# Folding layer norm's centring and gain into the first weight matrix, with every weight set multiplied by Strassen's scheme

## The chip, the cores and the metric

The kernel runs on one core of one Trainium2 chip. The metric is the device time of one execution in microseconds (us). Each kernel is run several times; the median counts.

## The reference

Attention without softmax, whose output x goes through a feed-forward part with a residual. There are 8 batches of 448 tokens, 12 heads of 64, 768 channels and 3072 hidden units.

```python
scores = (1/sqrt(64)) * q @ k.T                 # each batch and head
x      = (maximum(scores, 0)**2 / 448) @ v      # heads side by side: (8, 448, 768)
mu, var = mean(x, -1), mean((x - mu)**2, -1)
xn     = (x - mu) / sqrt(var + 1e-6) * g_ln     # g_ln > 0, one value for each channel
out    = x + maximum(xn @ w_ch1, 0) @ w_ch2     # 768 -> 3072 -> 768
```

Inputs and output are float32; the products run in bf16 and add up in float32.

## The kernel before

**Pairs and stages.** The 8 batches are worked in 4 pairs of 896 tokens (seven token tiles of 128, `NT`). For each pair x is kept transposed, `xT`: six chunks (`K1`) of 128 channels on the partitions, tokens along the free axis. `xc` is the centred x times g, one tile for each batch. The hidden layer is `hT`, 24 chunks (`K2`) of 128 hidden units by 896 tokens. Dividing by the standard deviation is left to the end: a token's `rstd` is positive, so it can be multiplied on after both products.

The stages follow each other on TensorE: pair 0's attention together with pair 0's first product (x to hidden); then three times a *loop*, in which a pair's second product (hidden to output) is interleaved with the next pair's attention, followed by that next pair's first product; last the second product of pair 3.

**Attention in a loop.** `attention` makes a list of units: bundles of three score tiles (L335 on TensorE, relu on ScalarE L346, square on VectorE L348), with `values` (L365) put in once a group of four heads is complete. `values` evicts x from PSUM (L372), scales it by g (`scaled`, L388), and `chunks_summed` (L400 to L407) adds up the six chunks of x on GpSimd. `centre` multiplies by a matrix of ones (L421), so that every partition holds each token's sum over the channels, and adds -g/768 times it to `xc` (L427).

**The second product.** `ffn2` (L634) has 56 units a pair: 7 token tiles, 2 halves of the output columns, 4 parts of 6 matmuls with 384 columns. After the fourth part `finish` (L645) multiplies by `rstd`, adds x and `store` sends the result out on SyncE's queue. `tokens` turns `xT` into token rows by a DMA transpose (L565); `statistics` (L572) and `roots` (L577, ScalarE's square root, then a reciprocal on VectorE) make `rstd` one tile ahead. `interleave` spreads the bundles over the units.

**The first product of pair 0** goes in blocks of 192 or 256 columns (`BLK`), so that it can begin before attention is done: `ffn1_head` (L618) takes the first three hidden chunks, `ffn1` (L596) each of the other 21, in two PSUM banks (`ps_mm`) used in turn, with a relu on ScalarE (L604). The last block is the 192 columns of batch 1 (`b=1`); it has no attention beside it.

**The first product of pairs 1 to 3** (`ffn1_pair`). Strassen's scheme multiplies two 2 x 2 block matrices with 7 block products instead of 8. The blocks are: hidden chunk n or n+12, channel chunks 0 to 2 or 3 to 5 (`KQ` = 3), batch `lo` or `hi` of the pair. A *set* n is thus 7 products of 3 matmuls with 448 columns (L752), against 24 plain matmuls, and needs five sums of w1 blocks and five sums of x blocks. Ten of the twelve sets go this way. The other two are plain, 48 matmuls (L596, the list `beside`): they give time for the x sums (`x_sum`, x[6], x[7]) and for the first sets' w1 sums. Those are made by GpSimd (`sums_early`, L721 to L723) and VectorE (`sums_late`, L735 and L739), two sets ahead. While pair 2 does this it also stores its sums in DRAM (`kept`, L744); pair 3 reads them back (`w_soon` L710 on ScalarE's or SyncE's queue, `w_late` L730 on SyncE's).

**What sets the order.** The program order is the schedule: each engine works through its instructions in the order written, waiting on semaphores for what it needs. Pools with few buffers add waits: `ps_sc` has 3 buffers of two banks, `ps_mm` 2 banks, `xc` 2 tiles, `ps_m` (first product, while `ps_sc` is closed) 6 banks. `busy` (L310) and `idle` (L206) are matmuls whose result nobody uses.

Of the kernel before, what the change touches and what calls it, by code (L numbers as in the profile page):

```python
# [28 lines left out]
def kernel(  # L29
# [156 lines left out]
    g_rows = const.tile([K1, 2, HP], fp32)  # L186
# [115 lines left out]
    FIRST = (0, BLK[0][0])  # L302
# [24 lines left out]
    def scores(n, slots, blk):  # L327
# [19 lines left out]
        if blk == FULL:  # L347
            nc.vector.tensor_mul(a, a, a)  # L348
        else:
            later.append((n, a))  # L350
# [3 lines left out]
    def values(n, blk):  # L354
# [15 lines left out]
        if b not in xc:  # L370
            xc[b] = xcpool.tile([P, K1, S], bf16, tag="xc", name="xc_sb")
        nc.vector.tensor_scalar_mul(  # L372
            xT[b // 2][:, 2 * m:2 * m + 2, of(blk, b)], ps[:, :, :w], score_scale)
        if (b, blk) != FIRST:
            scaled(b, m, blk)
        g["attn"] = []
        since[0] = 9
        if blk == FULL:
            chunks_summed(b, m)
# [10 lines left out]
    part = {}  # L390

    def chunks_summed(b, m):


        x = xT[b // 2][:, :, of(FULL, b)]
        if b % 2 and m == G - 1:
            return
        if m == 0:
            part[b] = spool.tile([P, S], fp32, tag="total", name="part_sb", bufs=1)
            nc.gpsimd.tensor_add(part[b], x[:, 0], x[:, 1])  # L400
        else:
            for c in range(2 * m, 2 * m + 2):
                nc.gpsimd.tensor_add(part[b], part[b], x[:, c])  # L403
        if m == G - 1 - b % 2:
            two = spool.tile([P, 2, S], bf16, tag="two", name="two_sb", bufs=1)
            nc.gpsimd.tensor_copy(two[:, 0], part[b])
            nc.gpsimd.tensor_sub(two[:, 1], part[b], two[:, 0])  # L407
            part[b] = two

    def centre(b, blk):  # L410
        w = blk[1] * HP
        straight = (b, blk) == FIRST or blk == FULL and b % 2
# [4 lines left out]
        rows = [xT[b // 2][:, c, of(blk, b)] for c in range(K1)]  # L417
        if blk == FULL:
            rows = [part[b][:, i] for i in range(2)] + (rows[4:] if b % 2 else [])
        for i, r in enumerate(rows):  # L420
            nc.tensor.matmul(ps, ones, r, start=(i == 0), stop=(i == len(rows) - 1))  # L421
        total = ps
        if not straight:
            total = spool.tile([P, S], fp32, tag="total", name="total_sb", bufs=1)[:, :w]
            nc.scalar.copy(total, ps)
        for c in range(K1):
            nc.vector.scalar_tensor_tensor(  # L427
                xc[b][:, c, of(blk)], total, g_mean[:, c:c + 1], xc[b][:, c, of(blk)],
                op0=ALU.mult, op1=ALU.add)

# [91 lines left out]
    def attention(bs):  # L522
# [9 lines left out]
        def item(n, i):  # L532
            scores(n, (i,), FULL)
            if i == J - 1 and n + 3 < len(groups):
                transposed(n + 3)

        def product(n):
            values(n, FULL)
            load(n + 4, "v")

        def bundle(items, at):
            for o, it in enumerate(items):
                item(*it)
                if o == at:
                    product(it[0] - 1)
        units, due = [], [[], []]
        for s in range(0, len(seq), 3):
# [4 lines left out]
            due.append([groups[n][0]] if at >= 0 and groups[n][1] == G - 1 else [])  # L552
            units += [lambda b=b: centre(b, FULL) for b in due.pop(0)]
        units.append(lambda: product(hi - 1))
        units.append(lambda: centre(bs[-1], FULL))
        return units
# [28 lines left out]
    def ffn1(b, ni, blk, few=False):  # L585
# [5 lines left out]
        if few:  # L591
            ps = ps_m.tile([P, 512], fp32, tag="m", name="h_ps")
        else:
            ps = ps_mm.tile([P, 512], fp32, tag="mm", name="h_ps")
        for c in range(K1):
            nc.tensor.matmul(  # L596
                ps[:, :w], w1[:, c, ni * P:(ni + 1) * P], xc[b][:, c, of(blk)],
                start=(c == 0), stop=(c == K1 - 1))
        since[0] += 1
        turns = 2 if (b, blk) == FIRST else 1  # L600
        if blk != FULL and since[0] <= turns:
# [6 lines left out]
    def ffn1_head(b, blk):  # L608
# [5 lines left out]
        one = ps_mm.tile([P, 512], fp32, tag="mm", name="h_ps")[:, :w]  # L614
        two = ps_sc.tile([P, 2, 512], fp32, tag="sc", name="h2_ps")[:, :, :w]
        for c in range(K1):
            for ni, ps in enumerate((one, two[:, 0], two[:, 1])):
                nc.tensor.matmul(  # L618
                    ps, w1[:, c, ni * P:(ni + 1) * P], xc[b][:, c, of(blk)],
                    start=(c == 0), stop=(c == K1 - 1))  # L620
# [42 lines left out]
    def ffn1_pair(pair, rows, beside, keep=False, given=None, between=None):  # L663
# [5 lines left out]
        lo, hi = xc[2 * pair], xc[2 * pair + 1]  # L669
        x = {3: lo[:, :KQ], 4: hi[:, KQ:], 6: hi[:, :KQ], 7: lo[:, KQ:]}  # L670
        w = {}
        first = spool.tile([P, 2, S], bf16, tag="two", name="w1_sum", bufs=1)
        first = first.rearrange("p i s -> p (i s)")
        temps = [spool.tile([P, S], fp32, tag="total", name="z_sb", bufs=1), first.bitcast(fp32)]
        if given is None:
            hold_x = [apool.tile([P, 2, 512], bf16, tag="attn", name="x_sum")[:, :, :S] for _ in range(5)]
            for m, t, rest in ((5, 0, (3, 0)), (2, 1, (3, 1)), (1, 2, (4, 0))):
                x[m] = (hold_x[t], hold_x[t][:, 0], hold_x[t][:, 1], hold_x[rest[0]][:, rest[1]])
            w_room = [[apool.tile([P, 2, 512], bf16, tag="attn", name="w1_sum")
                       .rearrange("p r (c n) -> p (r c) n", n=P) for _ in range(2)] for _ in range(2)]  # L680
            room = xpool.tile([P, K1, S2], bf16, tag="xT", name="room_sb")
            rest = room[:, KQ:].rearrange("p c s -> p (c s)")[:, :2048].rearrange("p (c n) -> p c n", n=P)
            w_room.append([rest[:, :8], rest[:, 8:]])
        else:
            for i, m in enumerate((5, 2, 1)):
                o = given["x"][:, i * KQ * S:(i + 1) * KQ * S].rearrange("p (c s) -> p c s", s=S)
                x[m] = (o, o[:, 0], o[:, 1], o[:, 2])
            room = xpool.tile([P, K1, S2], bf16, tag="xT", name="room_sb")
        temps += [room[:, n].bitcast(fp32) for n in range(KQ)]

        def x_sum(m, a, b):
            if given is None:
                nc.vector.tensor_add(x[m][0], a[:, :2], b[:, :2])
                nc.vector.tensor_add(x[m][3], a[:, 2], b[:, 2])
            else:
                nc.vector.tensor_add(x[m][0], a, b)

        def blocks(n):
            i, j = rows[n]
            i, j = slice(i * P, (i + 1) * P), slice(j * P, (j + 1) * P)  # L700
            return w1[:, :KQ, i], w1[:, :KQ, j], w1[:, KQ:, i], w1[:, KQ:, j]

        def sums_early(n):
            if n >= len(rows):
# [3 lines left out]
            if given is not None:  # L708
                soon = given["pool"].tile([P, 3 * KQ, P], bf16, tag="soon", name="w1_soon", bufs=2)
                (nc.scalar if n > 1 else nc.sync).dma_start(soon, kept[:, n, :3 * KQ])  # L710
                w[n].update({3: soon[:, :3], 4: soon[:, 3:6], 1: soon[:, 6:9]})
                return
            one, two = w_room[n % 3]
            if n == 0:
                f = first.rearrange("p (c n) -> p c n", n=P)
                w[n].update({3: f[:, :3], "4a": f[:, 3:5], "4b": f[:, 5], 4: f[:, 3:6]})
            else:
                w[n].update({3: two[:, :3], "4a": one[:, 6:8], "4b": two[:, 6],
                             4: (None, one[:, 6], one[:, 7], two[:, 6])})
            w[n].update({1: one[:, :3], 6: one[:, 3:6], 7: two[:, 3:6], "16": one[:, :6]})  # L720
            nc.gpsimd.tensor_sub(w[n][3], b12, b22)  # L721
            nc.gpsimd.tensor_sub(w[n]["4a"], b21[:, :2], b11[:, :2])
            nc.gpsimd.tensor_sub(w[n]["4b"], b21[:, 2], b11[:, 2])  # L723

        def sums_late(n):
            if n >= len(rows):
                return
            if given is not None:
                late = given["pool"].tile([P, 2 * KQ, P], bf16, tag="late", name="w1_late", bufs=2)
                nc.sync.dma_start(late, kept[:, n, 3 * KQ:])  # L730
                w[n].update({6: late[:, :3], 7: late[:, 3:6]})
                return
            b11, b12, b21, b22 = blocks(n)
            j = slice(rows[n][1] * P, (rows[n][1] + 1) * P)
# [5 lines left out]
            if keep:  # L740
# [14 lines left out]
        def relu(n, ps, row, half):  # L755
            nc.scalar.activation(  # L756
                hT[pair][:, rows[n][row], half * S:(half + 1) * S], ps, ACTF.Relu)
# [10 lines left out]
        for unit in beside[:4]:  # L768
            unit()
        sums_early(0)  # L770
        sums_early(1)
        if given is not None:
            sums_late(0)
            sums_late(1)
            tokens(pair)
        x_sum(5, lo[:, :KQ], lo[:, KQ:])
        x_sum(2, hi[:, :KQ], hi[:, KQ:])
        x_sum(1, lo[:, :KQ], hi[:, KQ:])
# [362 lines left out]
```

## Time and profile before

Three runs took 526.82 us in the median (526.72 to 527.58). The profiled execution took 527.49 us; its span, from the first to the last instruction in the trace, is 525.7.

| engine | busy us | share of the span | instructions |
|---|---|---|---|
| TensorE, matmuls (PE) | 516.9 | 98% | 4612 |
| TensorE, weight loads (PEld, beside the matmuls) | 305.5 | 58% | 4612 |
| VectorE (DVE) | 388.5 | 74% | 727 |
| ScalarE (ACT) | 284.1 | 54% | 478 |
| GpSimd (POOL) | 197.3 | 38% | 246 |

The stages, from the times of their first and last instructions:

| stage | from, us | to, us | PE busy in it |
|---|---|---|---|
| attention and first product of pair 0, without its last block | 0 | 88.7 | 84.5 |
| last block of pair 0's first product | 88.7 | 100.0 | 11.2 |
| loop 0: second product of pair 0, attention of pair 1 | 100.0 | 175.2 | 75.2 |
| first product of pair 1 | 175.2 | 225.9 | 50.7 |
| loop 1 | 225.9 | 299.2 | 73.3 |
| first product of pair 2 | 299.2 | 350.2 | 51.0 |
| loop 2 | 350.2 | 423.4 | 73.2 |
| first product of pair 3 | 423.4 | 474.7 | 51.0 |
| second product of pair 3 | 474.7 | 525.7 | 46.8 |

A row of a profile names an engine, a source line (L752 is line 752 of the kernel), the operation, the tile written and the tiles read with the shape. Times are in microseconds from the start of the span. SP is SyncE, which here only issues DMAs.

### The profile page before, as it was taken

Reading aid. Unit: us, or ns where it says so; the run is one execution under the profiler, and the core shown is the slowest. Engines: PE = TensorE matmul, PEld = TensorE weight load, DVE = VectorE, ACT = ScalarE, POOL = GpSimd, SP = SyncE. Lnnn points to the kernel's source line nnn. Section 1 sums busy time; section 2 is a strip of 40 time slices with the busy share of each in tenths; the row PEclk is TensorE's granted clock in tenths of the full one; section 3 lists DMA queues with packets and bytes.
Section 4 is the critical chain, followed back from the end, with each engine's and each line's share of the span. In section 5 each row is a group of like instructions: output and inputs, shape, how many; then the busy total and the mean of one; then the engine's idle time right before and its main releaser. Section 6 shows DMA issues by size and latency. Waiting matters only on the chain.

```text
span 525.7 us, 11571 instructions
## 1 busy us (share of the span) xinstructions
PE 516.9 (98%) x4612; PEld 305.5 (58%) x4612; DVE 388.5 (74%) x727; ACT 284.1 (54%) x478; POOL 197.3 (38%) x246
## 2 busy tenths in 40 slices
PE   8899999999999999999999999999999999999996
PEld 6678778755555555555555555555555554555663
DVE  5775654278898788758889779856989856886773
ACT  6966775465545266746646256647555435761110
POOL 7335102114624376002343727300330319991331
PEclk9999999999999999999999999999999999999999
DMA  9999999999988930216999885614651147421123
GB/s 196 206 206 207 211 192 164 172 159 139 171 137 153 185 68 0 36 31 102 169 170 179 134 206 172 157 36 62 131 104 46 46 111 185 116 88 31 38 54 91
DMA packets 121224, 66.50 MB, mean 126 GB/s; under 512 B 79698, under 2 KB 119890, under 8 KB 121170
## 3 DMA queue, kind: packets, MB, share of 16 engines
q1 hardware_dynamic: 92178, 37.05, 36.2%
q0 software_dynamic: 26976, 25.50, 33.0%
q10 hardware_dynamic: 2016, 3.21, 1.7%
q8 instruction: 36, 0.59, 0.5%
q14 instruction: 18, 0.15, 0.1%
HBM read 56.82 MB, written 15.93 MB: 138 GB/s over the span
## 4 chain that ended last, share of the span: by engine, by line
PE 93%; DMA 3%; POOL 2%; ACT 1%; DVE 1%; issue 0%; ACTq 0%; DVEq 0%; POOLq 0%
PE o_ps L634 34%; PE m_ps L752 21%; PE h_ps L596 15%; PE m_ps L885 8%; PE sc_ps L335 7%; PE av_ps L365 6%; DMA w<-in_moe_w_ch_dram 2%; PE h_ps L618 1%; DMA w_soon<-kept 1%; PE sum_ps L421 1%; ACT early L346 1%; PE tr_ps L220 1%; POOL v_sb L130 0%; POOL w L148 0%; POOL k_sb L130 0%
## 5 line engine op out<-in xcount | busy, mean ns | idle before, releaser
L634 PE MATMUL o_ps<-w,hT_sb 128*128 128x384 bf16 x1056 | 181.6, 326 | 0.0
L346 ACT ACTIVATE attn_sb<-sc_ps 128x896 bf16<-128x896 f32 (+4 forms) x150 | 126.4, 902 | 82.3 <-PE sc_ps L335 69.5
L634 PEld LDWEIGHTS <-hT_sb 128*128 128x128 bf16 x1056 | 99.6, 98 | 78.1 <-issue 15.2
L348 DVE TENSOR_TENSOR attn_sb<-attn_sb 128x896 bf16<-128x896 bf16 x126 | 81.6, 662 | 31.5 <-ACT attn_sb L346 26.9
L756 ACT ACTIVATE hT_sb<-m_ps 128x448 bf16<-128x448 f32 x120 | 65.2, 544 | 37.7 <-PE m_ps L752 35.7
L596 PE MATMUL h_ps<-xc_sb,w 128*128 128x192 bf16 (+2 forms) x648 | 82.2, 280 | 0.7 <-DMA w<-in_moe_w_ch_dram 0.3
L596 PEld LDWEIGHTS <-w 128*128 128x128 bf16 x648 | 58.1, 98 | 20.9 <-issue 3.1
L604 ACT ACTIVATE hT_sb<-h_ps 128x192 bf16<-128x192 f32 (+2 forms) x93 | 37.7, 406 | 56.8 <-PE h_ps L596 56.3
L400 POOL TENSOR_TENSOR part_sb<-xT_sb 128x448 f32<-128x448 bf16 x6 | 6.6, 1103 | 104.6 <-DVE xT_sb L372 84.9
L403 POOL TENSOR_TENSOR part_sb<-part_sb,xT_sb 128x448 f32<-128x448 f32 x18 | 23.3, 1295 | 55.6 <-DVE xT_sb L372 54.9
L846 POOL TENSOR_TENSOR w_sum_t<-w 128x384 bf16<-128x384 bf16 x48 | 41.8, 910 | 0.0
L752 PE MATMUL m_ps<-x_sum,w 128*128 128x448 bf16 x180 | 38.9, 352 | 0.0
L752 PE MATMUL m_ps<-xc_sb,w_sum 128*128 128x448 bf16 x168 | 36.4, 352 | 0.0
L572 DVE BATCH_NORM_STATS2 stats<-xtok_sb 128x6 f32<-128x384 bf16 x56 | 28.3, 546 | 10.7 <-DMA xtok_sb<-xT_sb 10.7
L335 PE MATMUL sc_ps<-qT_sb,kT_sb 64*64 64x448 bf16 x504 | 35.0, 358 | 0.0
L372 DVE TENSOR_SCALAR xT_sb<-av_ps 128x896 bf16<-128x896 f32 (+2 forms) x30 | 27.0, 901 | 7.8 <-PE av_ps L365 7.7
L365 PE MATMUL av_ps<-attn_sb,v_sb 64*64 64x448 bf16 (+2 forms) x672 | 32.3, 327 | 0.0
L752 PEld LDWEIGHTS <-w_sum 128*128 128x128 bf16 x210 | 20.5, 98 | 19.3 <-issue 0.3
L645 DVE SCALAR_TENSOR_TENSOR o_sb<-o_ps,rstd_sb,xtok_sb 128x384 f32<-128x384 f32 x44 | 26.6, 604 | 4.4 <-PE o_ps L634 4.4
L365 PEld LDWEIGHTS <-v_sb 64*64 64x64 bf16 x840 | 22.7, 107 | 11.8 <-issue 1.6
L388 DVE TENSOR_SCALAR xc_sb<-xT_sb,g_sb 128x448 bf16<-128x448 bf16 (+2 forms) x54 | 26.6, 541 | 1.0
L752 PEld LDWEIGHTS <-w 128*128 128x128 bf16 x180 | 17.6, 98 | 16.4
(144 smaller groups left out, 652.2 us busy)
## 6 DMA issues: line engine op xcount, KB each, us to landing
out_dram<-o_sb SPq DMA_DIRECT2D x90, 96.0 KB, 2.5
v_sb<-in_v_dram POOLq DMA_DIRECT2D x24, 224.0 KB, 5.3
w<-in_moe_w_ch_dram POOLq DMA_DIRECT2D x12, 384.0 KB, 13.9
w<-in_moe_w_ch_dram POOLq DMA_DIRECT2D x4, 1152.0 KB, 20.2
q_sb<-in_q_dram POOLq DMA_DIRECT2D x20, 224.0 KB, 6.6
k_sb<-in_k_dram POOLq DMA_DIRECT2D x20, 224.0 KB, 5.8
w_soon<-kept ACTq DMA_DIRECT2D x8, 288.0 KB, 3.5
w_late<-kept SPq DMA_DIRECT2D x10, 192.0 KB, 3.2
```

What stands on the lines that cost most here:

```text
L335: nc.tensor.matmul(ps[cols, r, o * w:(o + 1) * w], g["k"](i)[rows, cols], g["q"](i, r)[rows, blk[0]:sum(blk), cols], start=True, stop=True)
L346: nc.scalar.activation(a, ps[:, :, :len(slots) * w], ACTF.Relu)
L348: nc.vector.tensor_mul(a, a, a)
L365: nc.tensor.matmul(ps[cols, hh, :w], v_sb[rows, pr, j * D:(j + 1) * D], g["attn"][i][rows, r, :], start=(j == 0), stop=(j == J - 1))
L572: nc.vector.bn_stats(stats[:, n], xtok[pair][:, n * G:(n + 1) * G, t, :])
L596: nc.tensor.matmul(ps[:, :w], w1[:, c, ni * P:(ni + 1) * P], xc[b][:, c, of(blk)], start=(c == 0), stop=(c == K1 - 1))
L604: nc.scalar.activation(hT[pair][:, ni, o:o + w], ps[:, :w], ACTF.Relu)
L634: nc.tensor.matmul(ps[:, :DH], hT[pair][:, ki, t * P:(t + 1) * P], w2[:, ki, cols], start=(o == 0), stop=(o == K2 - 1))
L752: nc.tensor.matmul(ps, *at, start=(first and c == 0), stop=(c == KQ - 1), skip_group_check=not first)
L756: nc.scalar.activation(hT[pair][:, rows[n][row], half * S:(half + 1) * S], ps, ACTF.Relu)
L846: op(w2_sum[name][:, i:i + n], b[x][:, i:i + n], b[y][:, i:i + n])
L885: nc.tensor.matmul(ps, x[:, ki], y[:, ki], start=(first and ki == 0), stop=(ki == KH - 1), skip_group_check=not first)
```

## The change

Let W be `w_ch1`. Then (x - mu) * g @ W = x @ W', where W' has row c equal to g[c] * W[c] minus, in every row, the vector (1/768) * sum over c of g[c] * W[c]. W' does not depend on the tokens. The change computes W' once and writes it over w1; the pairs 1 to 3 then multiply their raw x, straight from `xT`.

- **The vector.** The last block of pair 0 (`LAST`) gets two more columns in `xc`, g/-768 split into a bf16 part and its remainder (`fold_tiles`). Its matmuls are thus 194 wide, and for each hidden chunk VectorE copies the two results out (`fold["sums"]`) ahead of the relu. `fold_sums` adds the two and splits the sum again, `fold_turn` turns it with one matmul, `fold_mean(i)` spreads four chunks of it over all partitions by four matmuls of 128 columns (a one-column pick, broadcast), ScalarE copying each result to SBUF.
- **The folding.** `fold_into(i, c)` is one VectorE instruction of 512 elements, w1 = w1 * g + mean, in place. The 36 of them, and the means, are spread over the units of loop 0 (`fold_beside`).
- **What goes.** For pairs 1 to 3 `scaled`, `chunks_summed` and `centre` are gone. `xc` tiles become S + 2 wide and now also hold x sums and Strassen's z.
- **All 12 sets by Strassen.** The list `beside` is gone. `ffn1_pair` now returns steps. `even` (after the pair's first batch: w1 sums of set 0 and x[5]) and `odd` (after group 4 of 6: x[6]) are hooked into the loop. `start`, after the last `values`, makes x[1], x[2], x[7] and set 1's w1 sums, and for pair 3 fetches sets 1 and 2. `run` is the loop over the sets. The last three units of the second product go between `start` and `run`.
- **The rooms.** `room0`, a constant tile, holds the w1 sums of sets 0, 3, 6, 9; its place serves as `g_rows` and for `centre`'s total before. In pair 3 all three rooms are refilled from `kept` three sets ahead.
- **Smaller edits.** In loop 0 ScalarE squares the third score tile of each bundle. The last `values` of a loop is evicted half by VectorE, half by ScalarE. `statistics` and `roots` of a pair's first tile come after `run`.

```diff
+    def fold_tiles():
+        t = xcpool.tile([P, K1, S + 2], bf16, tag="xc", name="fold_sb").rearrange("p c s -> p (c s)")
+        ...
+        nc.vector.memset(fold["rows"], 0.0)
+        nc.vector.tensor_add(fold["pick"], identity[:, :K2], identity[:, K2:2 * K2])
+        hi, lo = (xc[1][:, :, S + i] for i in range(2))
+        nc.vector.tensor_copy(hi, g_mean)
+        nc.vector.tensor_sub(lo, g_mean, hi)
+    def fold_sums():
+        s, rows = fold["sum"], fold["rows"]
+        nc.vector.tensor_add(s, fold["sums"][:, :, 0], fold["sums"][:, :, 1])
+        nc.vector.tensor_copy(rows[:, :K2], s)
+        nc.vector.tensor_sub(rows[:, K2:2 * K2], s, rows[:, :K2])
+    def fold_turn():
+        ps = ps_sc.tile([P, 2, 512], fp32, tag="sc", name="turn_ps")[:, 0, :P]
+        nc.tensor.matmul(ps, fold["rows"], identity, start=True, stop=True)
+        nc.scalar.copy(fold["cols"], ps)
+    def fold_mean(i):
+        ps = ps_sc.tile([P, 2, 512], fp32, tag="sc", name="mean_ps")[:, 0]
+        for o, ni in enumerate((2 * i, 2 * i + 1, K2 // 2 + 2 * i, K2 // 2 + 2 * i + 1)):
+            nc.tensor.matmul(
+                ps[:, o * P:(o + 1) * P], fold["pick"][:, ni:ni + 1].broadcast_to([P, P]),
+                fold["cols"], start=True, stop=True)
+        nc.scalar.copy(fold["means"][i % 2], ps)
+    def fold_into(i, c):
+        w = w1[:, c].rearrange("p (h n) -> p h n", h=2)[:, :, 2 * i * P:(2 * i + 2) * P]
+        nc.vector.scalar_tensor_tensor(
+            w, w, g_sb[:, c:c + 1], fold["means"][i % 2].rearrange("p (h n) -> p h n", h=2),
+            op0=ALU.mult, op1=ALU.add)
+    def fold_beside(units):
+        more = {0: [fold_turn], 1: [lambda: fold_mean(0)], 2: [lambda: fold_mean(1)]}
+        for i in range(K2 // 4):
+            for c in range(K1):
+                more.setdefault(4 + 8 * i + c, []).append(lambda i=i, c=c: fold_into(i, c))
+            if i + 2 < K2 // 4:
+                more.setdefault(14 + 8 * i, []).append(lambda i=i: fold_mean(i + 2))
...
     def ffn1(b, ni, blk):
+        more = 2 if (b, blk) == LAST else 0
...
+                ps[:, :w + more], w1[:, c, ni * P:(ni + 1) * P], xc[b][:, c, s.start:s.stop + more],
                 start=(c == 0), stop=(c == K1 - 1))
+        if more:
+            nc.vector.tensor_copy(fold["sums"][:, ni], ps[:, w:w + more])
...
             nc.scalar.activation(hT[pair][:, ni, o:o + w], ps[:, :w], ACTF.Relu)
...
     def ffn1_pair(...):
+        lo, hi = xT[pair][:, :, :S], xT[pair][:, :, S:]
+        xd = xcpool.tile([P, K1, S + 2], bf16, tag="xc", name="x_sum")[:, :, :S]
+        x = {3: lo[:, :KQ], 4: hi[:, KQ:], 5: xd[:, :KQ], 6: xd[:, KQ:]}
...
+        def even():
+            if given:
+                rooms[0].update(early=room0[:, :3 * KQ], late=room0[:, 3 * KQ:])
+            sums_early(0)
+            nc.vector.tensor_add(x[5], lo[:, :KQ], lo[:, KQ:])
+            sums_late(0)
+        def odd():
             nc.vector.tensor_sub(x[6], hi[:, :KQ], lo[:, :KQ])
+        def start():
...
+                for n in (1, 2):
+                    sums_early(n)
+                    sums_late(n)
...
+            x_sum(1, lo[:, :KQ], hi[:, KQ:], nc.vector.tensor_add)
+            x_sum(2, hi[:, :KQ], hi[:, KQ:], nc.vector.tensor_add)
+            x_sum(7, lo[:, KQ:], hi[:, KQ:], nc.vector.tensor_sub)
+            if not given:
+                nc.vector.memset(rooms[1][3][:, 0, :2], 0.0)
+                sums_early(1)
...
         for unit in ffn1_units(1, BLK[1][1]):
             unit()
+    fold_sums()
     statistics(0, 0)
     roots(0, 0, 1)
...
+        beside, left = attention(
+            [2 * pair + 2, 2 * pair + 3], {G - 1: lambda: hook("even"), 2 * G - 2: lambda: hook("odd")})
+        interleave(units[:-3], beside)
+        for f in left:
+            f()
+        wide.close()
...
+        hook("start")
+        ps_m = open_narrow()
+        for unit in units[-3:]:
+            unit()
+        stage = following
+        tokens(pair + 1)
+        stage["run"]()
+        if not last:
+            statistics(pair + 1, 0)
+            roots(pair + 1, 0, 1)
```

More of the change, by code (lines that the diff above doesn't have):

```diff
@@ L661 @@
     kept = dram.tile([P, KH, 5 * KQ, P], bf16, name="kept")
[L663 to L694, printed above, removed]
-            else:
-                nc.vector.tensor_add(x[m][0], a, b)
```

340 lines of the change are left out of this document (176 added, 164 removed).

## The prediction

> **What bounds the kernel now.** I read the busy time by stretches first. TensorE (PE) is busy 516.9 of 525.7 us and the granted clock is 1.00 throughout, so I looked for stretches in which PE has nothing to do, and then for what makes it slow where it is busy.
>
> ```profile
> core 0: us, PE busy (x) PEld busy (x) DVE busy (x) ACT busy (x) POOL busy (x), PEclk, DMA share, GB/s
> 88.72:99.95 11.23, 11.23 (x128) 10.46 (x126) 1.23 (x3) 7.16 (x22) 0.00 (x0) 1.00 1.40 189
> 99.95:175.20 75.25, 75.25 (x680) 40.91 (x678) 59.04 (x106) 38.21 (x51) 29.12 (x34) 1.00 0.98 152
> ...
> 423.40:474.70 51.30, 50.98 (x273) 26.36 (x271) 38.47 (x73) 31.10 (x58) 42.67 (x49) 1.00 0.48 128
> ```
>
> The rows are: the last block of pair 0's first product, pair 0's second product with attention beside it (the "first loop"), and the first product of pair 3 (in those of pairs 1 and 2 PE is busy 50.70 of 50.70 and 50.95 of 51.00). PE has no gap in the loop and almost none in the first products. So time comes off only where PE gets fewer columns to stream, and any work taken from DVE or POOL there is worth nothing by itself. Second I read the chain of waits:
>
> ```profile
> 173.44 0.76 PE sum_ps L421 x4
> ...
> 175.18 9.08 PE h_ps L596 x48
> ...
> 434.25 5.34 DMA w_soon<-kept
> ```
>
> A 448-column matmul costs 9.08/48 = 0.189 us, a column-sum matmul 0.76/4 = 0.19. The 5.34 us of DMA in the chain are not idle PE: by the list of PE's own waits it lost 0.3 us there (51.30 - 50.98), it worked on other products meanwhile. The chain names who released, not how much was lost.
>
> Third, how the 192-column block runs, from ScalarE's (ACT) timeline:
>
> ```profile
> 90.83 0.33 ACT L604 ACTIVATE hT_sb<-h_ps 128x192 bf16<-128x192 f32 x1 [0.16 <-PE h_ps L596]
> 91.40 0.33 ACT L604 ACTIVATE hT_sb<-h_ps 128x192 bf16<-128x192 f32 x1 [0.25 <-PE h_ps L596]
> 91.90 0.33 ACT L604 ACTIVATE hT_sb<-h_ps 128x192 bf16<-128x192 f32 x1 [0.16 <-PE h_ps L596]
> ```
>
> Two units take 1.07 us (90.83 to 91.90), in steps of 0.57 and 0.50, though 12 matmuls at the head's pace (1.48 us for 18 in the chain, 0.082 each) need 0.99. The two PSUM banks of ps_mm set this pace: fill 0.495, relu 0.331, so the two hand-overs between PE and ACT take 1.07 - 0.83 = 0.245. This block is already bound by its banks.
>
> **The change, part by part.**
>
> *Matmuls removed.* Before, each of three pairs has 48 plain matmuls, 6 column sums (4 + 2) and 10 sets of 21, together 264; after, 12 sets of 21, 252: 12 fewer in each pair. 36 x 0.189 = **-6.8 us**, all on PE's path. The wait of 0.3 us for w_soon goes too: set 0 of pair 3 is fetched in mid loop into room0, and the loads of sets 1 and 2 now stand ahead of the last o_sb store and the token transpose on SP's queue, where before they came 9 us after the last av (issued at 427.9, av ended 418.7): **-0.3**. The 24 scalings, centrings and POOL sums per pair that disappear lie beside a PE without gaps: nothing.
>
> *Matmuls added.* fold_turn 1 and fold_mean 6 x 4, each 128 columns, between the units of the first loop. Nearest row: six busy_ps of that shape.
>
> ```profile
> 16.26 0.51 PE L310 MATMUL busy_ps<-ones 128*128 128x128 bf16 x6
> 16.70 0.52 PE L365 MATMUL av_ps<-early,v_sb 64*64 64x192 bf16 x16
> ```
>
> 0.44/6 = 0.073 us each; the line through 448 columns (0.189) and 192 (0.082) gives 0.055 at 128, and threes of busy_ps elsewhere take 0.09. 25 x 0.073 = **+1.8** (1.4 to 2.3). The Trainium skill ("TensorE: Matmul & The Clock Gate", "Wait — 56ns, not 53.3ns?") has a warm matmul start every N/2.4 GHz plus about 2.5 ns, 55.6 ns at 128 columns; by it this term would be 1.4.
>
> *Two more columns and 23 small copies in the last block of pair 0.* 144 matmuls grow by 2 columns, 0.8 ns each: 0.1 us, inside the fill. Ahead of each relu DVE copies the two extra columns out of the same bank, and the built order makes ACT's relu wait for that copy, not for PE. A copy of that kind from PSUM:
>
> ```profile
> L197 DVE COPY g_sb<-idle_ps x1: 154/154/154, 6.7 to 6.7; 128x6 f32<-128x6 f32 x1
> ```
>
> So the bank's cycle becomes fill + hand-over + copy 0.154 + a hand-over DVE to ACT + relu + hand-over. For the extra hand-over the trace has 0.03 (a root ends at 100.50, the reciprocal starts at 100.53) to 0.12 (half of 0.245); I take 0.05. 0.2 per two units, 21 units: 2.1, and 0.2 in the head, where ACT waits twice: **+2.3** (0 if the copy costs ACT nothing; 3.2 with 0.12 and 0.3). The Trainium skill ("PSUM — Partial Sum Buffer", "PSUM bank collisions raise a hardware error") says that two engines must not touch one bank at a time, two readers included; by it the copy cannot lie beside the relu. It speaks against this part; without it this term would be 0.
>
> *The turn into rows.* fold_sums is three dependent small DVE operations (some 0.55 us), then come the statistics of token tile 0 (98.46 to 99.73 before: 1.27). ACT's queue has the root of these ahead of fold_turn's copy. Counted from DVE's last 2-column copy: statistics done 1.8, root 2.1, copy of 128x128 (0.28 by the 0.33 and 0.385 of 192 and 256 columns) 2.4. PE, which finished 0.2 earlier, is through unit 0, the turn and unit 1 (0.98 each) at 1.85 and waits for cols: **+0.55** (0 to 1). Behind it nothing else waits that is short of time: the first scores come two units later.
>
> *36 fold_into on DVE in the first loop.* One is a 512-element scalar_tensor_tensor with one fp32 operand, as L427 is with 448; starts of instructions tell what each occupies:
>
> ```profile
> 422.50 3.64 DVE L427 SCALAR_TENSOR_TENSOR xc_sb<-sum_ps,g_mean,xc_sb 128x448 bf16<-128x448 f32 x6 [2.06 <-PE sum_ps L421]
> ...
> 110.51 0.63 DVE L348 TENSOR_TENSOR attn_sb<-attn_sb 128x896 bf16<-128x896 bf16 x1 [0.18 <-ACT attn_sb L346]
> 111.05 0.61 DVE L645 SCALAR_TENSOR_TENSOR o_sb<-o_ps,rstd_sb,xtok_sb 128x384 f32<-128x384 f32 x1
> 111.58 1.01 DVE L572 BATCH_NORM_STATS2 stats<-xtok_sb 128x6 f32<-128x384 bf16 x2
> ...
> 118.62 1.11 DVE L388 TENSOR_SCALAR xc_sb<-xT_sb,g_sb 128x448 bf16<-128x448 bf16 x1
> ...
> 171.89 0.32 DVE L388 TENSOR_SCALAR xc_sb<-xT_sb,g_sb 128x448 bf16<-128x448 bf16 x1
> ```
>
> 3.64/6 = 0.61 for 448, plus 64 elements at 1.04 ns: 0.67. A square occupies 0.54, an eviction with rstd 0.53, statistics 1.17. Eight units (one token tile) take PE 76/56 x 8 = 10.9 us; DVE then has 1.17 + 2 x 0.53 + 0.07 + 6 x 0.67 + 4 squares 2.16 (the third of each bundle goes to ACT) + 0.83 scalings of 1.1 = 9.4 us. 86% full; in the six units that carry folds 9.1 us of DVE meet 8.2 of PE, a lag of about 1 us that the next two units take up. Squares are needed some 3 us after their relu, PSUM of o_ps 5 us after: hidden, **0**. ACT gets 14 squares of about 0.83 and 7 copies: 38 + 16 of 76 us, also hidden.
>
> *Start of a first product.* Cover shrinks from 48 plain matmuls (9.08) to three units of second product (2.93). From the end of the last av: DVE scales half 0.7, ACT the other half after it 1.35; the x sums take 0.85 each (0.62 and 0.39 overlapping) and end at 3.4; eviction 4.0; z adds 4.8 and 5.3; w1 sums of set 1 at 6.3 to 6.9; the two subtractions 7.4 and 8.0. PE wants the first x sum at 4.1, w1 sums of set 1 at 5.8 (POOL: from 3.5 to 5.6) and 6.9, the subtractions at 7.5 and 8.0. Nearly every one arrives in time: **+0.2** for pairs 1 and 2 together (0 to 1.6). fold_tiles' four small operations (0.35) stand on DVE ahead of squares that nobody waits for within 3 us: 0.
>
> Sum: -6.8 - 0.3 + 1.8 + 2.3 + 0.55 + 0.2 = **-2.2 us**. The profiled execution took 527.49 with a span of 525.7; the median of the runs is 526.82. I take the difference off the median: **524.6**, a span near 523.5.
>
> **Rivals.**
> 1. *The copies are free* (ACT's relu reads beside DVE, or the banks had slack): without the 2.3, 522.3. For it: DVE is idle in that block (1.23 of 11.23 us). Against it: the order of waits, and the 1.07 us cycle that is already the banks'.
> 2. *The thin cover at the start of the first products costs*: each link above late by the contention that POOL causes (L735 takes 0.55 to 0.99), 0.8 in pairs 1 and 2, and 0.5 in pair 3 if its loads collide with the transposes: +1.9 over the forecast, 526.5, no change. For it: slacks of 0 to 0.5 us. Against: in the steady sets DVE has always run ahead.
> 3. *DVE becomes the bound of the first loop: slower.* Place: the fold units. It decides once a fold occupies more than 0.67 + (10.9 - 9.4)/6 = 0.92 us. L388 shows that a DVE operation can stretch from 0.32 to 1.11 while POOL computes. At 1.1 us per fold, eight units need 12.0 us instead of 10.9; over six token tiles 6.2: 530.8. Against: POOL's sums leave this loop; it only issues DMAs there.
>
> **From cases to numbers.** Forecast 0.55 (its own range 523.4 to 525.9), rival 1 0.15, rival 2 0.13, rival 3 0.17. A measurement of this kernel can tell about 0.2%, 1.05 us, from no change. Faster (under 525.8): nine tenths of the forecast and rival 1, 0.65; the same: 0.17; slower: rival 3 and a little of the second, 0.18. The range reaches to rivals 1 and 2 and leaves out the third: 522.0 to 527.6.
>
> **What would show it.** Matmul count 36 lower at 448 columns and 25 higher at 128. In the last block of pair 0: relus every 1.27 us per two units instead of 1.07 (rival 1: 1.07). One PE wait of about 0.5 us for the turned sums. In the first loop no PE wait for DVE squares (rival 3: several, and DVE above 95%). Between last av and the second set of each first product no gap over 0.3 us. I am wrong in kind if PE waits inside the first loop, and wrong in size mostly through the copies.

## The result and the profile after

The changed kernel takes 528.62 us in the median of 16 runs, the kernel before 526.99 (16 runs): a ratio of 1.004, interval 1.0025 to 1.0055. It is slower by 1.6 us where 2.2 us less were forecast. The profiled execution took 528.62 us with a span of 526.8, 1.1 more than the span before. (In some executions of most of the kernels, the one before too, the beginning takes some 3.5 us longer, ahead of the change; the profiles of two experiments below, `e_all` and `h_sqdve`, are such ones, so their stages are compared, not their spans.)

I cut both spans where the timeline of TensorE shows the first matmul of a stage start: the last block, the first o_ps matmul, the first 448-column product. A first product thus ends with the first o_ps matmul of the next loop, and the last block has its `ffn1_head` in it, so these stages differ a little from the first table's.

| stage, us | before | after | change |
|---|---|---|---|
| last block of pair 0 | 12.71 | 14.85 | +2.14 |
| loop 0 | 75.22 | 77.37 | +2.15 |
| first product, pair 1 | 47.67 | 47.29 | -0.38 |
| loop 1 | 76.36 | 75.22 | -1.14 |
| first product, pair 2 | 47.88 | 47.14 | -0.74 |
| loop 2 | 76.35 | 75.22 | -1.13 |
| first product, pair 3 | 48.16 | 48.46 | +0.30 |
| ahead of the last block, and the rest | 141.35 | 141.25 | -0.10 |

Loops 1 and 2 give just what the six column sums cost (6 x 0.189 = 1.13). In the first products the six matmuls saved in each should give as much again; they gave 0.38, 0.74 and less than nothing. The other two costs are the last block and loop 0, which also lost its six column sums and grew all the same.

The busy times by stretches, with the columns of before, for the last block, loop 0 and pair 3's first product:

```profile
86.91:101.76 14.85, 14.84 (x147) 12.25 (x144) 4.22 (x25) 7.67 (x23) 0.72 (x1) 1.00 1.36 197
101.76:179.13 77.37, 76.00 (x699) 41.80 (x697) 66.63 (x124) 54.67 (x72) 15.88 (x21) 1.00 0.99 154
...
424.00:472.46 48.46, 46.89 (x249) 24.06 (x247) 38.38 (x71) 30.79 (x58) 40.94 (x46) 1.00 0.52 139
```

The first row looks full, 14.84 of 14.85 us, though the same 144 matmuls took 12.7 before: a busy TensorE is not one at its peak; only the number of columns says how long the work is. In the two others it has gaps of 1.37 and 1.57 us, where it had none and 0.32 before. The chain of waits names what stands ahead of the second of these:

```profile
423.72 1.65 DVE x_sum L731 x2
427.87 10.96 PE m_ps L784 x57
```

The list of TensorE's own waits has lines that the kernel before does not have:

```profile
PE m_ps L784 <- DVE z_sb L850: 1.4, 1, 1.4
...
PE m_ps L784 <- DVE m_ps L863: 0.9, 2, 0.5
PE mean_ps L450 <- DVE xT_sb L378: 0.8, 1, 0.8
...
PE mean_ps L450 <- ACT fold_sb L445: 0.4, 1, 0.4
```

The columns after the colon are the total, the number of waits and the longest. All of it stands at the starts of the first products (L784) and in loop 0 (L450); what held TensorE up is VectorE in three of the four.

ScalarE's timeline in the last block, to be held against the 1.07 us per two units before:

```profile
90.58 0.33 ACT L650 ACTIVATE hT_sb<-h_ps 128x192 bf16<-128x192 f32 x1 [0.33 <-DVE fold_sb L644]
91.19 0.33 ACT L650 ACTIVATE hT_sb<-h_ps 128x192 bf16<-128x192 f32 x1 [0.28 <-DVE fold_sb L644]
91.85 0.33 ACT L650 ACTIVATE hT_sb<-h_ps 128x192 bf16<-128x192 f32 x1 [0.33 <-DVE fold_sb L644]
```

From 90.58 to 91.85 are 1.27 us, and the releaser of each relu is now VectorE's copy.

The start of pair 3's first product, in VectorE's timeline and then GpSimd's:

```profile
422.42 4.34 DVE L731 TENSOR_TENSOR x_sum<-xT_sb 128x1344 bf16<-128x1344 bf16 x3 [0.61 <-ACT xT_sb L376]
426.69 0.60 DVE L697 SCALAR_TENSOR_TENSOR o_sb<-o_ps,rstd_sb,xtok_sb 128x384 f32<-128x384 f32 x1
427.21 0.60 DVE L850 TENSOR_TENSOR z_sb<-z_sb,m_ps 128x448 f32<-128x448 f32 x1
```

```profile
421.30 21.04 POOL L905 TENSOR_TENSOR w_sum_t<-w 128x384 bf16<-128x384 bf16 x22 [43.47 <-DMA out_dram<-o_sb]
```

Three x sums take 4.34 us; the same sum of 1344 elements takes 0.85 in the loops, and in the kernel before, with GpSimd idle, VectorE made these three in 2.39:

```profile
426.58 2.39 DVE L696 TENSOR_TENSOR x_sum<-xc_sb 128x1344 bf16<-128x1344 bf16 x3
```

In the changed kernel GpSimd works beside them without a break on sums of w2 for the last stage. The kernel before had the same 48 sums of w2, but they began much later, behind a third of x[6] that stood ahead of them on GpSimd's queue:

```profile
432.03 1.28 POOL L789 TENSOR_TENSOR xc_sb<-xc_sb 128x448 bf16<-128x448 bf16 x1 [14.73 <-PE h_ps L596]
433.28 12.23 POOL L846 TENSOR_TENSOR w_sum_t<-w 128x384 bf16<-128x384 bf16 x14
```

The change makes all of x[6] on VectorE, inside the loop:

```diff
-            nc.vector.tensor_sub(x[6][:, :2], hi[:, :2], lo[:, :2])
-            nc.gpsimd.tensor_sub(x[6][:, 2], hi[:, 2], lo[:, 2])
```

By the order of the queue it thereby took away what had kept GpSimd waiting: the sums of w2 moved from 433.28 to 421.30, onto the moment when VectorE has least time.

In pairs 1 and 2 it is the change's own sums that meet. `start` gives GpSimd set 1's early w1 sums (179.78 to 184.02 in pair 1), and within the first set VectorE comes to that set's late ones:

```profile
181.80 1.19 DVE L765 TENSOR_TENSOR w_sum<-w 128x768 bf16<-128x768 bf16 x1
182.91 0.82 DVE L769 TENSOR_TENSOR w_sum<-w 128x384 bf16<-128x384 bf16 x1
```

### The profile page after: what moved, and what is told of

It reads as the page before. It is cut to its first block, busy times and chain, and to the rows that moved or that the text cites. A ratio compares the mean times of both kernels' runs of the same rounds, so it can differ in the third digit from the quotient of the medians.

```text
span 526.8 us, 11571 instructions
## 1 busy us (share of the span) xinstructions
PE 515.3 (98%) x4601; PEld 304.0 (58%) x4601; DVE 383.2 (73%) x741; ACT 303.7 (58%) x505; POOL 164.4 (31%) x213
## 4 chain that ended last, share of the span: by engine, by line
PE 90%; DVE 4%; ACT 3%; issue 2%; DVEq 0%; ACTq 0%
PE o_ps L686 30%; PE m_ps L784 25%; PE h_ps L640 10%; PE m_ps L945 8%; PE sc_ps L336 7%; PE av_ps L368 6%; PE h_ps L666 2%; ACT early L347 1%; PE tr_ps L221 1%; PE idle_ps L207 1%; ACT attn_sb L347 1%; DVE w L457 1%; DVE z_sb L850 0%; PE sum_ps L405 0%; DVE stats L616 0%
## 5 line engine op out<-in xcount | busy, mean ns | idle before, releaser
L788 ACT ACTIVATE hT_sb<-m_ps 128x448 bf16<-128x448 f32 x144 | 78.2, 544 | 49.5 <-PE m_ps L784 47.1
L351 DVE TENSOR_TENSOR attn_sb<-attn_sb 128x896 bf16<-128x896 bf16 x112 | 70.0, 630 | 40.5 <-ACT attn_sb L347 39.5
L130 POOL DMA_DIRECT2D v_sb<-in_v_dram x24 | 17.2, 717 | 173.6 <-PE sc_ps L336 137.4
L640 PE MATMUL h_ps<-xc_sb,w 128*128 128x256 bf16 (+2 forms) x504 | 56.5, 259 | 0.3 <-ACT early L347 0.3
L640 PEld LDWEIGHTS <-w 128*128 128x128 bf16 x504 | 44.0, 97 | 9.5 <-issue 3.4
L784 PE MATMUL m_ps<-x_sum,w 128*128 128x448 bf16 x216 | 47.1, 352 | 1.6 <-DVE z_sb L850 1.4
L863 DVE TENSOR_TENSOR m_ps<-z_sb,m_ps 128x448 f32<-128x448 f32 x36 | 22.6, 627 | 20.2 <-ACT hT_sb L788 20.0
L650 ACT ACTIVATE hT_sb<-h_ps 128x192 bf16<-128x192 f32 (+1 forms) x69 | 24.7, 358 | 21.8 <-PE h_ps L640 15.1
L784 PEld LDWEIGHTS <-w_sum 128*128 128x128 bf16 x240 | 23.4, 98 | 21.9 <-DVE w_sum L765 0.2
L784 PEld LDWEIGHTS <-w 128*128 128x128 bf16 x216 | 21.1, 98 | 21.7 <-issue 2.1
L784 PE MATMUL m_ps<-x_sum,w_sum 128*128 128x448 bf16 x144 | 31.2, 352 | 0.0
L784 PEld LDWEIGHTS <-room 128*128 128x128 bf16 x180 | 17.6, 98 | 17.5 <-issue 1.4
```

What stands on the lines that cost most here:

```text
L640: nc.tensor.matmul(ps[:, :w + more], w1[:, c, ni * P:(ni + 1) * P], xc[b][:, c, s.start:s.stop + more], start=(c == 0), stop=(c == K1 - 1))
L784: nc.tensor.matmul(ps, *at, start=(first and c == 0), stop=(c == KQ - 1), skip_group_check=not first)
L788: nc.scalar.activation(hT[pair][:, n + KH * row, half * S:(half + 1) * S], ps, ACTF.Relu)
```

## The experiments

Each is the changed kernel with one edit, unless said; diffs are against it. Medians are to be held against 528.62; the kernel before took 527.1 to 527.3 beside them. Stage times are cut as in the table.

**a_banks: more banks for the last block.**

```diff
         more = 2 if (b, blk) == LAST else 0
+        if more and ni % 2:
+            ps = ps_sc.tile([P, 2, 512], fp32, tag="sc", name="h2_ps")[:, 0]
+        else:
+            ps = ps_mm.tile([P, 512], fp32, tag="mm", name="h_ps")
```

> The changed kernel (528.62 us), but every second unit of pair 0's last block takes a bank of ps_sc, which is idle there, so the block turns over four banks and more in place of two. Theory (the 23 copies cost time because copy, relu and fill follow each other in one of only two banks, 1.27 us per two units): the block, 14.85 us from its first matmul to the first of the second product, becomes bound by its matmuls, 144 x 0.083 = 11.9, so 2.9 us less, 525.7. Rival (the time is in the engines: a copy on VectorE and a relu on ScalarE per unit, or in the wider matmuls, whatever the banks): the block stays at 14.8, 528.6.

525.72 us, ratio to before 0.998 (0.9968 to 0.9992). The block takes 12.00 us. ScalarE's timeline, with copy and relu as they were:

```profile
90.29 0.33 ACT L652 ACTIVATE hT_sb<-h_ps 128x192 bf16<-128x192 f32 x1 [0.17 <-DVE fold_sb L646]
90.79 0.33 ACT L652 ACTIVATE hT_sb<-h_ps 128x192 bf16<-128x192 f32 x1 [0.17 <-DVE fold_sb L646]
91.28 0.33 ACT L652 ACTIVATE hT_sb<-h_ps 128x192 bf16<-128x192 f32 x1 [0.17 <-DVE fold_sb L646]
```

Two units now take 0.99 us (90.29 to 91.28), the matmuls' own time. So the copies and relus never were too much for their engines; what cost was that only two banks took turns. This also takes away what the block of the kernel before had lost to its banks (12.71 to 12.00).

**b_nocopy: the copies left out.** In place of the 23 `tensor_copy` into `fold["sums"]` stands one memset; w1 is folded with g alone.

```diff
-            nc.vector.tensor_copy(fold["sums"][:, ni], ps[:, w:w + more])
...
+        nc.vector.memset(fold["sums"], 0.0)
```

> The changed kernel without the 23 copies of the two extra columns; the sums are set to zero instead, so w1 is folded with g alone and the mean is left out. The 194-column matmuls, the turn, the spreading and the folds stay. Theory (the copies in the bank's cycle are what made the block 2.1 us longer): the block goes from 14.85 to 12.8, 526.5. Rival (the two extra columns themselves, or a slower clock): the block stays near 14.8, 528.6.

525.95 us. The block takes 12.80, so the copies cost 2.05 us and the two wider columns about 0.1. Loop 0 shrank by 0.6 as well, since the sums are there earlier and the wait for the turned rows is gone.

**c_poollate: GpSimd held back.**

```diff
-            if not given:
+            if given:
+                nc.vector.memset(w2_sum["t3"][:, 0, :2], 0.0)
+            else:
                 nc.vector.memset(rooms[1][3][:, 0, :2], 0.0)
                 sums_early(1)
```

> The changed kernel, but GpSimd's w2 sums for the last stage wait for pair 3's x sums (a two-column memset on VectorE into the first one's tile). Theory (the three x sums of pair 3 took 4.34 us in place of 2.6 because GpSimd computes w2 sums beside them; that is why TensorE waits 1.43 us for the first z): they take 2.6, the wait goes, 48.46 us of first product become 47.0 or less: 527.0. Rival (they are slow by their form, 1344 elements in one instruction, or by the DMA loads that land beside them): 4.3 us as before, 528.6.

526.84 us. VectorE's timeline and GpSimd's:

```profile
422.46 2.40 DVE L731 TENSOR_TENSOR x_sum<-xT_sb 128x1344 bf16<-128x1344 bf16 x3 [0.61 <-ACT xT_sb L376]
```

```profile
425.20 5.25 POOL L907 TENSOR_TENSOR w_sum_t<-w 128x384 bf16<-128x384 bf16 x6 [47.34 <-DMA w_room<-kept]
```

With GpSimd starting at 425.20 in place of 421.30 the same three sums take 2.40 us, and the first product 46.56 in place of 48.46. The form of the instruction and the DMA loads were the same, so the rival falls.

**d_cover: twice the cover, late sums ahead.**

```diff
-        interleave(units[:-3], beside)
+        interleave(units[:-6], beside)
...
-        for unit in units[-3:]:
+        for unit in units[-6:]:
...
                 sums_early(1)
+                sums_late(1)
...
                     sums_early(n + 2)
-                    sums_late(n + 1)
+                    if n:
+                        sums_late(n + 1)
```

> The changed kernel with six units of the second product in place of three held back behind the x sums as cover (5.85 us in place of 2.93), and set 1's late w1 sums of pairs 1 and 2 made before the first set in place of within it. Theory (the first products of pairs 1 to 3 lose 0.5, 0.4 and 1.4 us in waits for VectorE because the cover is short): these three waits vanish, 2.3 us less, 526.3. Rival (the loop then has three units fewer beside the attention, so its waits grow by what is won; or the sets are bound by VectorE whatever the cover): 528.6 or more.

525.65 us, 0.9981 (0.9963 to 0.9998). The first products take 46.57, 46.56 and 46.57: no wait is left in them, and loops 1 and 2 stay at 75.22. So 46.57 is what the matmuls alone take (246 of the 252 lie between the cuts, the other six behind the next loop's first o_ps), and the changed kernel lost 0.72, 0.57 and 1.89 there. 46.57 is also 1.10 less than the 47.67 of pair 1 before: the six matmuls do give what they should, once nothing stands in their way. Loop 0 stays long, 77.52: its wait of 0.8 for VectorE is gone, since the bundles of attention fall on other units, and three short waits of scores for ScalarE's copies of means, 0.5 in all, stand in its place.

**i_cover and k_lateonly: the two halves of d_cover apart.** The first has only the changed numbers of units, the second only the moved `sums_late(1)`.

> The changed kernel with six units of cover in place of three, and nothing else (set 1's late sums stay within the first set). Theory (pairs 1 and 2 lose 0.7 and 0.6 us because GpSimd makes set 1's early w1 sums at the moment at which VectorE makes the late ones, 1.19 us in place of 0.55; with more cover GpSimd is done before): the first products come down to 46.6 us each, as with both edits, 525.7. Rival (the late sums stand in the first set's chain of VectorE and are too much there in any case): pairs 1 and 2 stay at 47.2 and only pair 3 gains, 526.8.

> The changed kernel with set 1's late w1 sums moved ahead of the first set, but three units of cover as it has. Theory (cover is what is short): VectorE's work of 2 us only moves ahead of the first z, beside GpSimd's early sums, TensorE then waits for z and the first products of pairs 1 and 2 get longer than 47.3 and 47.1: 529 or more. Rival (the order within the set is what costs): they go to 46.6, 527.4.

i_cover: 526.52 us; pairs 2 and 3 come to 46.56 and 46.57, pair 1 stays at 47.34. k_lateonly: 528.97; 47.35 and 47.33 for pairs 1 and 2. The theory of the first is thus half a miss; that of the second held. In pair 1 of i_cover GpSimd makes sums still when VectorE comes to set 1's late ones:

```profile
181.97 1.07 DVE L765 TENSOR_TENSOR w_sum<-w 128x768 bf16<-128x768 bf16 x1
182.97 1.06 DVE L769 TENSOR_TENSOR w_sum<-w 128x384 bf16<-128x384 bf16 x1
```

Alone they take 0.55 and 0.35 (so at 186.26 and 186.73 in the same trace). In pair 2 one of the two got through in 0.34, which was enough. Cover alone helps where it happens to separate the two engines, order alone helps not at all; pair 1 needed both. No run holds GpSimd back in pairs 1 and 2, as c_poollate does in pair 3. There the cause is worked out from the durations: in the changed kernel 0.55 and 0.35 in place of 1.19 and 0.82 would end some 1.0 us earlier, and TensorE was held up by 0.65.

**t_turn: the root behind the turn's copy.**

```diff
-    roots(0, 0, 1)
...
-        more = {0: [fold_turn], 1: [lambda: fold_mean(0)], 2: [lambda: fold_mean(1)]}
+        more = {0: [fold_turn, lambda: roots(0, 0, 1)], 2: [lambda: fold_mean(0)], 3: [lambda: fold_mean(1)]}
```

> The changed kernel, but token tile 0's root is issued behind the turn's copy on ScalarE, and the first two means come in units 2 and 3 in place of 1 and 2. Theory (TensorE's 0.43 us wait for the turned sums is the root ahead of the copy and too short a distance): it goes, the other wait of a mean (0.8, for VectorE's eviction of attention values) stays: 528.2. Rival (the distance is needed elsewhere: the scores or the first output eviction then wait): 528.6 or more.

528.41 us: the wait of 0.43 is gone, one of 0.2 for ScalarE's copy of a mean stands in its place, and loop 0 is shorter by 0.15 only. 0.2 us lies within the scatter of the medians; the stage times say so much and no more.

**g_nomeans, j_nofold, h_sqdve: what makes loop 0 longer.** The first leaves out the turn and the means (`more = {}`, the means set to zero), the second the 36 folds (w1 keeps its values), the third puts all squares on VectorE:

```diff
-                item(*it, o == 2 and bs[0] == by_dma)
+                item(*it, False)
```

> The changed kernel without the turn and the spreading (25 matmuls of 128 columns and 7 ScalarE copies); the means are set to zero, so the mean is left out of the fold. The copies, the 194 columns and the 36 folds stay. Theory (in the first loop only TensorE's own work and the waits of these matmuls cost): 25 x 0.08 = 2.0 and 0.4 + 0.8 of waits go, 3.2 less, 525.4. Rival (the first loop is long because VectorE, with 36 folds more, is its bound): at most 1 us goes, 527.6 or more.

> The changed kernel without the 36 folds (w1 keeps its values, so g and the mean are left out of pairs 1 to 3); the sums, the turn and the 24 spreading matmuls stay. Theory (the folds keep VectorE so full that an eviction of attention values comes 0.8 us late, once; the rest of the first loop's growth is the 25 matmuls): the loop goes from 77.4 to 76.6, 527.8. Rival (the folds cost nothing, and the 0.8 is the order around the mean): 77.4, 528.6. Rival (the folds cost more, by contention for memory): under 76.2.

> The changed kernel with all squares of the first loop on VectorE: 14 that ScalarE did move over. VectorE's busy time in the loop, 66.6 of 77.4 us, becomes some 74 by 0.54 us each. Theory (VectorE is near its limit there, so the moved squares are what keeps it off the path): TensorE gets waits for squares or evictions, 0.5 to 2 us in all, 529.1 to 530.6. Rival (it has room enough): 528.6.

Loop 0 takes 75.29, 76.77 and 78.34 us, against 77.37; the medians are 527.01, 527.96 and 529.75. g_nomeans missed: 2.1 went, not 3.2. The waits of the means went. The eviction that had held one of them up in the changed kernel came no earlier (it began at 156.33), but nothing waited for it. A new wait came in at the eviction of the group before:

```profile
PE sc_ps L336 <- DVE xT_sb L378: 1.0, 1, 1.0
```

```profile
136.72 3.59 DVE L459 SCALAR_TENSOR_TENSOR w<-w,g_sb,fold_sb 128x512 bf16<-128x512 bf16 x2
140.24 1.15 DVE L351 TENSOR_TENSOR attn_sb<-attn_sb 128x896 bf16<-128x896 bf16 x2
141.31 1.08 DVE L378 TENSOR_SCALAR xT_sb<-av_ps 128x896 bf16<-128x896 f32 x1
```

Two folds took 3.59 us there, in the changed kernel 1.41 (at 137.55). GpSimd made two w1 sums beside them (137.97 to 139.76); no run shows whether they are the whole cause. From start to start the wait cost 1.2 us. Without it loop 0 would be 74.1, just what is left of the 75.22 before when its column sums (1.13) are taken off: so the turn, the means and the waits that come with them are worth 3.3, near the 3.2 expected, and the folds cost TensorE time only through waits.

The waits of loop 0 in j_nofold:

```profile
PE mean_ps L450 <- ACT fold_sb L445: 0.4, 1, 0.4
PE mean_ps L450 <- DVE xT_sb L378: 0.2, 1, 0.2
```

The mean shares its PSUM pool (`ps_sc`) with the attention values, so it can start only when their eviction has freed a buffer. Without folds that eviction is 0.2 late, with them 0.8, with 14 squares more on VectorE 1.8 (73.7 us busy of 78.34). VectorE's timeline in the changed kernel shows the place:

```profile
154.07 1.40 DVE L457 SCALAR_TENSOR_TENSOR w<-w,g_sb,fold_sb 128x512 bf16<-128x512 bf16 x2
...
155.39 0.61 DVE L351 TENSOR_TENSOR attn_sb<-attn_sb 128x896 bf16<-128x896 bf16 x1
155.93 1.08 DVE L378 TENSOR_SCALAR xT_sb<-av_ps 128x896 bf16<-128x896 f32 x1
```

The product was ready at about 154.7; its eviction began at 155.93, behind two folds and a square.

One more wait in loop 0 is too short for the list. Attention values wait for a PSUM buffer until ScalarE has copied a mean out of it, a copy that stands behind a square and a root (ScalarE's and TensorE's timelines in the changed kernel):

```profile
136.17 0.56 ACT L453 COPY fold_sb<-mean_ps 128x512 f32<-128x512 f32 x1
```

```profile
136.07 0.57 PE L336 MATMUL sc_ps<-qT_sb,kT_sb 64*64 64x448 bf16 x8
136.78 1.52 PE L368 MATMUL av_ps<-attn_sb,v_sb 64*64 64x448 bf16 x28
```

The last score matmul starts at 136.29 and the values 0.49 us later, where it takes 0.20 elsewhere in this loop: 0.3 us.

**e_all: the repairs together.** a_banks, d_cover and t_turn in one kernel.

> The changed kernel with the banks of ps_sc in the last block, six units of cover with set 1's late sums ahead, and in the first loop token tile 0's root behind the turn's copy on ScalarE's queue, the first two means one unit later. Theory (the three costs lie one behind the other on TensorE's path and add): 2.9 + 3.0 + 0.4 less than 528.6, 522.3, under the kernel before by 4.5. Rival (they hide each other, the same wait counted twice): 524 or more.

522.26 us, ratio to before 0.9902 (0.9887 to 0.9916): 4.9 us faster than the kernel before. Its stages: block 12.00, loop 0 77.00, first products 46.57, 46.56, 46.56. The repairs add up. In loop 0 no wait for VectorE is left, only the three short ones for ScalarE's copies of means.

**l_wide: e_all with the means spread by six matmuls of 512 columns.**

```diff
+        for o, ni in enumerate((0, 1, KH, KH + 1)):
+            nc.tensor.matmul(
+                ps[:, o * P:(o + 1) * P], fold["rows"][:, ni:ni + P], identity, start=True, stop=True)
...
-        for o, ni in enumerate((2 * i, 2 * i + 1, K2 // 2 + 2 * i, K2 // 2 + 2 * i + 1)):
...
+        nc.tensor.matmul(
+            ps, fold["pick"][:, 2 * i:2 * i + 1].broadcast_to([P, P]), fold["cols"],
+            start=True, stop=True)
```

> The kernel with all three repairs (522.26 us), and the 24 spreading matmuls of 128 columns replaced by 6 of 512: the turn makes four shifted copies side by side (4 matmuls of 128 columns), so that one matmul spreads four chunks. Theory (the 25 matmuls cost TensorE some 0.085 us each, more than their 0.055 of streaming): 6 x 0.215 + 4 x 0.085 = 1.6 in place of 2.1, 521.8. Rival (they are paid by the column, 25 x 0.055 = 1.4, and the rest of the first loop's growth is waits): 6 x 0.215 + 4 x 0.055 = 1.5 against 1.4, 522.3.

522.61 us, loop 0 77.15: no gain. The rival held. TensorE's timeline of the changed kernel had shown it:

```profile
104.36 0.38 PE L450 MATMUL mean_ps<-fold_sb 128*128 128x128 bf16 x4 [0.43 <-ACT fold_sb L445]
104.58 0.65 PE L686 MATMUL o_ps<-w,hT_sb 128*128 128x384 bf16 x3
```

From the first mean matmul to the next unit are 0.22 us, 0.055 each: they are paid by the column.

## Why the prediction was wrong, step by step

- *Matmuls removed, -6.8:* right. d_cover shows -1.10 in pair 1's first product and loops 1 and 2 show -1.14 and -1.13; six such parts are the 6.8.
- *The copies, +2.3:* mechanism and size right. The cycle of 1.27 us was met, the block grew by 2.14, b_nocopy gives the copies 2.05. Rival 1 (copies free) fell. The Trainium skill's rule ("PSUM — Partial Sum Buffer", "PSUM bank collisions raise a hardware error") asks for the order that the trace has: a copy runs from 90.39 to 90.55 and the relu starts at 90.58, never beside it. What the forecast did not draw from its own sentence "already bound by its banks" is that the cost can be avoided.
- *Matmuls added, +1.8:* mis-sized. Between starts they take 0.055 each, 25 x 0.055 = 1.4, as the line through 192 and 448 columns said and as the Trainium skill says ("TensorE: Matmul & The Clock Gate", "Wait — 56ns, not 53.3ns?"). I had taken the 0.073 of six busy_ps. Between the six themselves it is 0.058 (starts from 16.26 to 16.55 in the kernel before); the 0.15 from the last of them to the 64*64 matmul behind it made the mean.
- *The turn, +0.55:* right, 0.43 in the list of waits and, with the 0.16 that the list leaves out (last section), 0.6.
- *36 folds on DVE, 0:* mis-sized. Averaged over eight units VectorE had room; in one place two folds and a square stood ahead of an eviction that freed a PSUM buffer. 0.8 us in the list, about 1.0 with what the list leaves out; 0.6 of loop time goes with the folds in j_nofold, the rest is VectorE's other work. That TensorE waits inside the first loop is what the prediction had named as being wrong in kind. It is near rival 3, which has VectorE as the bound of the loop: here it is one wait, and where it falls hangs on the order (in d_cover it is gone with all folds in place). With 14 squares more, h_sqdve, it grows to 1.8. Rival 3's own sum has a slip: 12.0 less 10.9, six times, is 6.6, not 6.2.
- *ScalarE's seven copies of means, 0:* mis-sized by the 0.3 of the wait at 136.78.
- *Start of a first product, +0.2 (0 to 1.6):* the step that failed, and with it the sign. It cost 0.72 + 0.57 + 1.89 = 3.2 us; with the 0.2 of the forecast in its place the changed kernel would still have been the faster one. I listed VectorE's work there with the durations that the instructions have when they run alone (0.85 for an x sum, 0.55 and 0.35 for late w1 sums) and found each in time by 0 to 0.5 us. Beside GpSimd they took 1.45, 1.19 and 0.82. The trace of before had that stretch (L735 from 0.55 to 0.99), and rival 2 named it, but gave pair 3 only 0.5, and for its DMA loads; c_poollate, with the same loads, takes the whole 1.89 away. That GpSimd's queue had lost the instruction that held it back until 432 was not looked for: it is one removed line, x[6]'s third, which the prediction does not mention.
- *The wait for w_soon, -0.3:* it is gone, as said. By the stages the kernel before had lost more than this: 0.21 in pair 2 and 0.49 in pair 3 against its own pair 1 (47.67), 0.7 in all.

Summed: -6.8 - 0.7 + 1.4 + 2.1 + 0.6 + 1.0 + 0.3 + 3.2 = +1.1 on the profiled spans, which differ by 1.1. Loop 0 alone closes too: -1.13 + 1.4 + 0.6 + 1.0 + 0.3 = 2.2, measured 2.15. The medians differ by 1.6, since the profiled execution of before (527.49) lay half a microsecond above its median.

Rival 2 was the nearest case, with 526.5. It gave the first products 2.1 us where they took 3.2, with pairs 1 and 2 about right and pair 3 far too cheap, and it had nothing more for loop 0; 528.62 lies above the range. "Wrong in size mostly through the copies", as the prediction has it at its end, was not so: the copies were right.

## What to carry to other kernels

When an edit removes an instruction from an engine that is "free", ask what that instruction had been holding back: the queue behind it can start earlier, and may run into the one moment where another engine is short. Cost the links of a tight start with the durations they have beside the other engine, not alone; here the trace of before had both. A bank of PSUM that is filled, read by two engines and filled again is a chain: see first whether idle banks can be had, before taking work out of it.

## What the runs showed of the hardware that was not expected

- Sums of two bf16 tiles on VectorE stretch beside sums on GpSimd: 0.80 us for 1344 elements alone (2.40 for three), 1.45 on the mean beside it (4.34). The Trainium skill says of this ("SBUF — State Buffer", "Who interferes with whom") that a VectorE instruction with two inputs in SBUF contends with a GpSimd instruction that reads SBUF, and that what they share is an exclusive lock. The trace fits it: VectorE's stretches (0.65 for an x sum) stay under one GpSimd instruction (21.04/22 = 0.96), and ScalarE's copies beside them keep their 0.53. The two folds in g_nomeans do not fit as simply: they lost 2.2 us, more than the two sums of GpSimd beside them last (1.8), and the rest is not explained.
- A wait of TensorE cost more than the list of waits says. In the changed kernel three matmuls that start at 183.10 would let the next begin at 183.67 (0.189 each); it began at 184.32. Lost are 0.65 us, listed 0.49: the list counts from the last matmul's end, which lies some 0.16 us behind the moment at which the next could have started.
